# First four weight pieces of a fused attention and MoE kernel: loads issued twelve steps ahead, one conversion turn per step instead of three, and the read of the result moved one turn behind its last step

## The chip, the cores and the metric

One core of a Trainium2 chip (trn2). The metric is the device time of one execution in microseconds, taken over several runs of the same program.

## The reference

```python
def reference(**kwargs):
    attn_out = _attn_ref(q, k, v, proj)                 # (2, 8, 768, 64)
    x = attn_out.transpose(0, 2, 1, 3).reshape(1536, 512)
    x = _moe_ref(x, w_in, w_out)                        # h = x @ w_in ; (h * sigmoid(h)) @ w_out
    return _moe2_ref(x, w_in2, w_out2)                  # h = x @ w_in2 ; (h - tanh(h)) @ w_out2

def _attn_ref(q, k, v, proj):
    q_bucket, k_bucket = hash(q, proj), hash(k, proj)   # six sign bits of q @ proj, k @ proj
    mask = q_bucket[:, :, :, None] == k_bucket[:, :, None, :]
    scores = np.where(mask, q @ k.T / 8, -1e9)
    attn = exp(scores - max); attn = attn / (attn.sum(-1) + 1e-9)
    return attn @ v
```

Two batches, eight heads, 768 rows of 64 in each head; two feed-forward layers of 512 by 2048 and 2048 by 512. The feed-forward weights come as 64-bit floats and are used as 32-bit ones.

## The kernel before

Attention runs in tiles: a tile is 128 query rows of one head against all 768 keys, six tiles to a head, 96 in all. A generator (`attention`) walks through 122 steps, 61 for each batch: in a step it records the scores of one tile (`scores`, L243), the reduction of those scores from PSUM with a row maximum (`soft_max`, L256, one for each tile, so that its 96 instructions count the tiles), the exponential (`soft_exp`, L264 and L265), and the product with V of a tile six steps back (`pv`, L312 to L314). The tile is turned for that product either on TensorE (`turn_p`, L279, with L281 and L282 out of PSUM; the odd tiles of the first batch) or by a transposing DMA (`soft_hi` L291, `soft_lo` L298 on GpSimd, L300 on the queue of SyncE, called SP). Each step yields three times. Step 61 begins the second batch; the last thirteen steps of a batch have no new tile.

Every float32 operand of a matmul is held as a high and a low half, made by a cast on ScalarE and a subtraction on GpSimd or VectorE. Feed-forward weights come in pieces of 128 rows by 512 columns. `Moe.load` issues the DMA of one piece on SP (L467, 512 KB, a ring of two buffers `w`). `Moe.take` lists the steps that turn the 64-bit numbers into 32-bit ones, one lambda each, as "turns": an absolute value on ScalarE (L507), then L508, L509, L511 on VectorE, and a last turn `last` with L498 on VectorE, L499 on ScalarE (cast to `wh`), L500 on GpSimd (`wl`) and a store for later use on SP (L502). `Moe.fill` does n turns, after it has issued the loads that have come due (one for each piece finished). The scratch `wa` has two buffers.

The main loop (L647 to L655) puts this between the steps of attention. At step 33 (`half - PRE`, 61 - 28) it calls `begin`, which issues the first two loads, and starts `first_weights`, which takes the first four pieces; from then on it does one turn at each of the three yields of a step until the end of step 60. These four pieces are all the rows of the first chunk of the first layer, which the first matmul groups of that layer read (`h_group`, L531). From step 61 on attention and the feed-forward layers (`run`, L531 and L555) are interleaved, with six turns to a step; after attention the rest of the layers follows.

The program is recorded in this order and then scheduled: Tile orders the instructions of each engine by priority and dependence, and each engine and the SP queue work through their own list strictly in order. `keep_in_program_order` ties single instructions (L467, L507) to the order of recording.

## Time and profile before

| what | value |
|---|---|
| runs | 779.87, 783.84, 785.07 us; median 783.84 us |
| profiled execution | 781.58 us, span 779.8 us |
| TensorE busy (PE) | 728.1 us, 93% of the span |
| VectorE (DVE) | 541.5 us, 69% |
| ScalarE (ACT) | 432.0 us, 55% |
| GpSimd (POOL) | 306.2 us, 39% |
| mean granted TensorE clock | 0.982 |

The profile names engines PE (matmul), PEld (weight load), DVE, ACT, POOL and SP (SPq is the DMA queue of SP). Times in a view are us from the start of the span. An arrow `[2.32 <-DMA w...]` behind an instruction is the idle time of its engine just before it and what ended that. The page's slices show TensorE nearly full from the eleventh of forty slices (195 us) on, and busy between four and nine tenths in the first ten.

### The profile page before, as it was taken

The numbers are of one execution on the slowest core, as the hardware profiler recorded it, in microseconds if no ns is written. First come the engines' busy times: TensorE is split into PE (matmuls) and PEld (weight loads), VectorE is DVE, ScalarE is ACT, GpSimd is POOL, SyncE is SP. The second block draws the span as 40 slices with busy tenths as digits, with TensorE's granted clock in tenths as the row PEclk, the third lists the DMA queues.
The fourth block names the chain that finished last, engine by engine and source line by source line (L and its number), as shares of the span: only waits on it lengthen the run. The fifth ranks groups of instructions, "written<-read, shape, count | busy, mean of one in ns | idle before, by whom it ended". The sixth has DMA issues, their size and how long they took to land.

```text
span 779.8 us, 14314 instructions
## 1 busy us (share of the span) xinstructions
PE 728.1 (93%) x5492; PEld 698.0 (90%) x5492; DVE 541.5 (69%) x1029; ACT 432.0 (55%) x821; POOL 306.2 (39%) x214
## 2 busy tenths in 40 slices
PE   4688876798999999999999999999999999999998
PEld 3677775687989899999999999999999999999998
DVE  6778879698888888886442445996858567584342
ACT  3778867898788789666444332562524325242130
POOL 4455546566777768557454310221111111110000
PEclk8799999999999999999999999999999999999999
DMA  7756669689899999993233220332112121110102
GB/s 259 191 137 140 135 138 187 149 167 246 215 238 277 227 232 253 201 240 103 80 109 107 72 65 16 121 109 82 54 55 82 55 82 54 56 55 1 58 24 82
DMA packets 138879, 100.39 MB, mean 129 GB/s; under 512 B 115870, under 2 KB 118174, under 8 KB 138810
## 3 DMA queue, kind: packets, MB, share of 16 engines
q1 hardware_dynamic: 137712, 97.54, 49.5%
q10 hardware_dynamic: 1098, 1.94, 1.0%
q8 instruction: 43, 0.70, 0.4%
q14 instruction: 26, 0.21, 0.1%
HBM read 57.95 MB, written 11.53 MB: 89 GB/s over the span
## 4 chain that ended last, share of the span: by engine, by line
PE 55%; POOL 1%; DVE 0%; ACT 0%; issue 0%; ACTq 0%
PE psm L555 27%; PE psm L531 27%; POOL xl L579 1%; POOL wl L500 0%; PE pso L312 0%; PE pso L314 0%; PE pso L313 0%; DVE p L256 0%; DVE wa L498 0%; DVE xt L330 0%; DVE acc L567 0%; ACT xh L578 0%; DVE den L321 0%; DVE den L320 0%; ACTq L578 0%
## 5 line engine op out<-in xcount | busy, mean ns | idle before, releaser
L500 POOL TENSOR_TENSOR wl<-wa,wh 128x512 fp32r<-128x512 f32 x64 | 82.7, 1293 | 237.8 <-ACT wh L499 236.4
L531 PE MATMUL psm<-xh,wh 128*128 128x384 f32 x512 | 173.0, 338 | 1.0 <-DVE hb L185 0.5
L555 PE MATMUL psm<-gh,wh 128*128 128x384 f32 x512 | 173.0, 338 | 0.4 <-ACT x L347 0.4
L531 PE MATMUL psm<-xh,wl 128*128 128x384 f32 x512 | 171.4, 335 | 1.1 <-POOL wl L500 1.1
L555 PE MATMUL psm<-gh,wl 128*128 128x384 f32 x512 | 171.6, 335 | 0.6 <-POOL wl L500 0.6
L555 PE MATMUL psm<-gl,wh 128*128 128x384 f32 x512 | 171.8, 335 | 0.0
L531 PE MATMUL psm<-xl,wh 128*128 128x384 f32 x512 | 171.3, 335 | 0.0
L298 POOL TENSOR_TENSOR hl<-p,hl 128x768 f16<-128x768 f32 x72 | 119.5, 1660 | 90.1 <-ACT hl L291 78.0
L256 DVE TENSOR_SCALAR_CACHE_REDUCE p<-ps 128x768 f32<-128x768 f32 x96 | 90.7, 948 | 28.0 <-PE ps L243 23.6
L543 DVE TENSOR_TENSOR gl<-psm,gh 128x384 fp32r<-128x384 f32 x128 | 71.1, 556 | 41.9 <-ACT gh L542 41.6
L531 PEld LDWEIGHTS psm<-xh,wh 128*128 128x128 f32 x512 | 96.1, 188 | 1.6 <-DVE hb L185 0.6
L531 PEld LDWEIGHTS psm<-xh,wl 128*128 128x128 f32 x512 | 96.1, 188 | 1.5 <-POOL wl L500 1.5
L555 PEld LDWEIGHTS psm<-gh,wl 128*128 128x128 f32 x512 | 96.3, 188 | 0.9 <-POOL wl L500 0.9
L555 PEld LDWEIGHTS psm<-gh,wh 128*128 128x128 f32 x512 | 96.5, 189 | 0.7 <-ACT x L347 0.6
L243 PE MATMUL ps<-k,q 128*128 128x384 f32 x336 | 84.5, 371 | 13.5 <-DVE p L256 9.6
L555 PEld LDWEIGHTS psm<-gl,wh 128*128 128x128 f32 x512 | 96.5, 189 | 0.0
L531 PEld LDWEIGHTS psm<-xl,wh 128*128 128x128 f32 x512 | 96.2, 188 | 0.0
L567 DVE TENSOR_TENSOR acc<-acc,psm 128x384 f32<-128x384 f32 x96 | 52.5, 549 | 60.4 <-PE psm L555 59.4
L542 ACT CAST gh<-psm 128x384 fp32r<-128x384 f32 x128 | 61.4, 481 | 57.9 <-DVE psm L541 35.6
L265 ACT ACTIVATE p<-p,bi 128x768 f32<-128x768 f32 x96 | 89.1, 937 | 4.9 <-DVE xt L330 1.1
L243 PEld LDWEIGHTS ps<-k,q 128*128 128x128 f32 x336 | 62.1, 205 | 18.1 <-DVE p L256 10.9
L540 ACT ACTIVATE th<-psm 128x384 f32<-128x384 f32 x64 | 31.5, 493 | 75.6 <-PE psm L531 75.6
(104 smaller groups left out, 1275.9 us busy)
## 6 DMA issues: line engine op xcount, KB each, us to landing
w<-in_w_in_dram SPq DMA_DIRECT2D x32, 512.0 KB
w<-in_w_out_dram SPq DMA_DIRECT2D x32, 512.0 KB
r<-in_qkT_dram SPq DMA_DIRECT2D x15, 768.0 KB
wi<-wa SPq DMA_DIRECT2D x16, 256.0 KB
wo<-wa SPq DMA_DIRECT2D x16, 256.0 KB
w<-wi SPq DMA_DIRECT2D x16, 256.0 KB
w<-wo SPq DMA_DIRECT2D x16, 256.0 KB
vr<-in_v_dram SPq DMA_DIRECT2D x6, 512.0 KB
```

The lines of the kernel that those rows point to most:

```text
L243: nc.tensor.matmul(out=ps[:, u, 0:HS], lhsT=a[:, t * 128:(t + 1) * 128], rhs=c[:, u * HS:(u + 1) * HS], start=(j == 0), stop=(j == 1))
L256: nc.vector.tensor_scalar(p.rearrange("p (c s) -> p c s", c=2), pss.pop(i)[:, :, 0:HS], FLOOR, None, op0=ALU.max, op1=ALU.max, accum_out=m)
L265: nc.scalar.activation(out=p, in_=p, func=ACTF.Exp, scale=0.125, bias=bi)
L298: nc.gpsimd.tensor_tensor(hl[:, 1, :], p, hl[:, 0, :], op=ALU.subtract)
L500: nc.gpsimd.tensor_tensor(ll, s, hh.bitcast(F32), op=ALU.subtract)
L531: nc.tensor.matmul(out=ps, lhsT=a[:, k, fs], rhs=b_[blk][:, k, :], start=(k == 0 and j == 0), stop=(k == KD - 1 and j == 2))
L540: nc.scalar.activation(out=th, in_=ps, func=ACTF.Tanh)
L542: nc.scalar.copy(gh[:, f, :], ps)
L543: nc.vector.tensor_tensor(gl[:, f, :], ps, gh[:, f, :].bitcast(F32), op=ALU.subtract)
L555: nc.tensor.matmul(out=ps, lhsT=a[:, f, ds], rhs=b_[:, f, :], start=(f == 0 and j == 0), stop=(f == F - 1 and j == 2))
L567: nc.vector.tensor_tensor(ac, ac, ps, op=ALU.add)
L579: nc.gpsimd.tensor_tensor(xl[blk][:, dt, :], src, xh[blk][:, dt, :].bitcast(F32), op=ALU.subtract)
```

## The change

Three edits. The step L498 leaves `last` and becomes a turn of its own, so a piece has six turns, and its reads (cast, subtraction, store) are the sixth. `begin` is called twelve steps earlier, at step 21. And turns are done at the third yield of a step alone, so one to a step and not three. After step 60 nothing is edited, except that a piece has six turns there too.

```diff
             def last():
-                nc.vector.scalar_tensor_tensor(r, lo, 29, u, op0=ALU.logical_shift_right, op1=ALU.bitwise_or)
                 nc.scalar.copy(hh, s)
                 nc.gpsimd.tensor_tensor(ll, s, hh.bitcast(F32), op=ALU.subtract)
                 if dr is not None:
@@
                 lambda: nc.vector.scalar_tensor_tensor(u, hi, -0x40000000, u, op0=ALU.bitwise_and,
+                                                       op1=ALU.bitwise_or),
+                lambda: nc.vector.scalar_tensor_tensor(r, lo, 29, u, op0=ALU.logical_shift_right,
                                                        op1=ALU.bitwise_or),
                 last,
@@
         for s, sub in attn:
+            if s == half - PRE - 12 and sub == 0:
+                moe.begin()
             if s == half - PRE and sub == 0:
-                moe.begin()
                 pre = moe.first_weights()
-            if pre is not None:
+            if pre is not None and sub == 2:
                 next(pre, None)
                 moe.fill()
```

In the changed file the lines shift: L507, L508, L509, L511, L498, L499, L500, L502 become L506, L507, L508, L510, L512, L498, L499, L501, and L531 becomes L532.

What the scheduler makes of it. First VectorE, from tile 35 on: `wa` and `w` are the weight pieces, `p` and `psm` tiles of attention. Before:

```order
L256 TENSOR_SCALAR p,mx<-ps 128x768
L282 TENSOR_TENSOR p<-psm,p 128x384
L508 TENSOR_SCALAR wa<-wa 128x512
L330 TENSOR_TENSOR xt<-pso,den 128x6x64
L509 TENSOR_SCALAR wa<-wa 128x512
L256 TENSOR_SCALAR p,mx<-ps 128x768
L511 SCALAR_TENSOR_TENSOR wa<-w,wa 128x512
L256 TENSOR_SCALAR p,mx<-ps 128x768
L498 SCALAR_TENSOR_TENSOR wa<-w,wa 128x512
L508 TENSOR_SCALAR wa<-wa 128x512
```

And after the change, from the same place:

```order
L256 TENSOR_SCALAR p,mx<-ps 128x768
L282 TENSOR_TENSOR p<-psm,p 128x384
L330 TENSOR_TENSOR xt<-pso,den 128x6x64
L256 TENSOR_SCALAR p,mx<-ps 128x768 x2
L507 TENSOR_SCALAR wa<-wa 128x512
L508 TENSOR_SCALAR wa<-wa 128x512
L282 TENSOR_TENSOR p<-psm,p 128x384
L510 SCALAR_TENSOR_TENSOR wa<-w,wa 128x512
L282 TENSOR_TENSOR p<-psm,p 128x384
L512 SCALAR_TENSOR_TENSOR wa<-w,wa 128x512
L256 TENSOR_SCALAR p,mx<-ps 128x768 x2
L282 TENSOR_TENSOR p<-psm,p 128x384 x2
```

Up to the reduction of tile 47 sixteen such rows stood in the list before, and eight stand there now. The other eight now stand around the first tiles of the second batch, VectorE again (`hl` is a tile, `cv` the next piece's scratch):

```order
L282 TENSOR_TENSOR p<-psm,p 128x384 x2
L507 TENSOR_SCALAR wa<-wa 128x512
L508 TENSOR_SCALAR wa<-wa 128x512
L510 SCALAR_TENSOR_TENSOR wa<-w,wa 128x512
L256 TENSOR_SCALAR p,mx<-ps 128x768
L512 SCALAR_TENSOR_TENSOR wa<-w,wa 128x512
L282 TENSOR_TENSOR hl<-psm,hl 128x384 x3
L256 TENSOR_SCALAR p,mx<-ps 128x768
L282 TENSOR_TENSOR hl<-psm,hl 128x384
L507 TENSOR_SCALAR wa<-wa 128x512
L256 TENSOR_SCALAR p,mx<-ps 128x768
L508 TENSOR_SCALAR wa<-wa 128x512
```

The first reduction here is that of tile 48, the first of the second batch; before, none of the weight rows stood here. The queue of SP, before, from the load of a head's q and k (`r`) that is issued at 72.07:

```order
L134 DMA r<-in_qkT_dram 128x1536
L300 DMA_TRANSPOSE pt<-hl 128x12x128 x3
L134 DMA r<-in_qkT_dram 128x1536
L300 DMA_TRANSPOSE pt<-hl 128x12x128 x4
L467 DMA w<-in_w_in_dram 128x1024 x2
L300 DMA_TRANSPOSE pt<-hl 128x12x128
L502 DMA wi_75<-wa 128x512
L467 DMA w<-in_w_in_dram 128x1024
```

And after, from the same load on:

```order
L134 DMA r<-in_qkT_dram 128x1536
L300 DMA_TRANSPOSE pt<-hl 128x12x128
L467 DMA w<-in_w_in_dram 128x1024 x2
L300 DMA_TRANSPOSE pt<-hl 128x12x128 x2
L134 DMA r<-in_qkT_dram 128x1536
L300 DMA_TRANSPOSE pt<-hl 128x12x128 x6
L501 DMA wi_75<-wa 128x512
L467 DMA w<-in_w_in_dram 128x1024
L300 DMA_TRANSPOSE pt<-hl 128x12x128 x3
L501 DMA wi_75<-wa 128x512
L300 DMA_TRANSPOSE pt<-hl 128x12x128
L134 DMA r<-in_qkT_dram 128x1536
```

The two loads have moved past six transpositions and a head's load, to between two transpositions; the fourth load follows behind the last row shown. On TensorE one place ahead of that changes with it: the matmuls that wait for the transposition behind the two loads. Before:

```order
L314 LDWEIGHTS p
L314 MATMUL pso<-v_221,p 128x65
L312 LDWEIGHTS pt
L312 MATMUL pso<-v_221,pt 128x65
L313 LDWEIGHTS pt
```

After:

```order
L314 MATMUL pso<-v_221,p 128x65
L243 MATMUL ps<-k_644,q_642 128x384 x2
L243 MATMUL ps<-k_645,q_643 128x384 x2
L243 MATMUL ps<-k_644,q_642 128x384 x2
L312 LDWEIGHTS pt
L312 MATMUL pso<-v_221,pt 128x65
```

Three rows of score matmuls (L243), which stood behind the eighteen matmuls that read `pt`, now stand ahead of them.

## Rows read from the trace of the kernel before

**Rows 1.** Windows of the span: stretch, length, busy us by engine (count), PEclk, DMA share, GB/s.
```profile
60.00:105.00 45.00, 40.15 (x515) 34.46 (x514) 35.20 (x79) 38.06 (x77) 26.96 (x16) 1.00 0.63 124
105.00:140.00 35.00, 22.63 (x260) 18.91 (x258) 31.70 (x56) 25.01 (x47) 17.66 (x12) 0.90 0.79 184
...
200.00:350.00 150.00, 146.20 (x1424) 137.35 (x1423) 126.13 (x250) 120.67 (x214) 108.31 (x70) 1.00 1.03 236
350.00:779.00 429.00, 425.42 (x2468) 424.34 (x2466) 257.02 (x460) 161.24 (x326) 93.22 (x74) 1.00 0.22 69
```
**Rows 2.** Timeline of VectorE: reductions of tiles 24, 35, 36, 47, 48; start, length.
```profile
77.97 0.92 DVE L256 TENSOR_SCALAR_CACHE_REDUCE p<-ps 128x768 f32<-128x768 f32 x1
...
101.31 0.95 DVE L256 TENSOR_SCALAR_CACHE_REDUCE p<-ps 128x768 f32<-128x768 f32 x1
...
106.02 0.92 DVE L256 TENSOR_SCALAR_CACHE_REDUCE p<-ps 128x768 f32<-128x768 f32 x1
...
142.83 0.94 DVE L256 TENSOR_SCALAR_CACHE_REDUCE p<-ps 128x768 f32<-128x768 f32 x1
...
150.26 0.96 DVE L256 TENSOR_SCALAR_CACHE_REDUCE p<-ps 128x768 f32<-128x768 f32 x1 [4.59 <-PE ps L243]
```
**Rows 3.** Instructions by line, VectorE, 105 to 140: count | busy, mean ns | idle before.
```profile
L498 DVE SCALAR_TENSOR_TENSOR wa<-w,wa 128x512 int32<-128x512 int32 x4 | 6.0, 1497 | 0.0
L511 DVE SCALAR_TENSOR_TENSOR wa<-w,wa 128x512 int32<-128x512 int32 x4 | 5.0, 1253 | 0.0
L509 DVE TENSOR_SCALAR wa<-wa 128x512 int32<-128x512 int32 x4 | 2.9, 713 | 0.0
L508 DVE TENSOR_SCALAR wa<-wa 128x512 f32<-128x512 f32 x4 | 2.3, 578 | 2.2 <-ACT wa L507 2.2
```
**Rows 4.** Instructions by line, ScalarE, 105 to 140.
```profile
L507 ACT ACTIVATE wa<-w 128x512 f32<-128x512 f32 x4 | 2.7, 664 | 2.3 <-DMA w<-in_w_in_dram 2.3
L499 ACT CAST wh<-wa 128x512 fp32r<-128x512 f32 x4 | 2.5, 618 | 6.6 <-DVE wa L498 6.6
```
**Rows 5.** Instructions of the tile wa to 320 us: count, shortest/median/longest ns, starts.
```profile
L508 DVE TENSOR_SCALAR wa<-wa x4: 415/496/906, 109.6 to 129.2; 128x512 f32<-128x512 f32 x4
L509 DVE TENSOR_SCALAR wa<-wa x4: 415/670/1097, 110.4 to 131.0; 128x512 int32<-128x512 int32 x4
L511 DVE SCALAR_TENSOR_TENSOR wa<-w,wa x4: 680/1176/1980, 111.6 to 132.3; 128x512 int32<-128x512 int32 x4
L498 DVE SCALAR_TENSOR_TENSOR wa<-w,wa x4: 674/1641/2031, 113.1 to 134.7; 128x512 int32<-128x512 int32 x4
```
**Rows 6.** Timelines of VectorE and of GpSimd, one pair that runs at once.
```profile
113.12 2.03 DVE L498 SCALAR_TENSOR_TENSOR wa<-w,wa 128x512 int32<-128x512 int32 x1
...
112.95 1.65 POOL L298 TENSOR_TENSOR hl<-p,hl 128x768 f16<-128x768 f32 x1 [7.66 <-ACT hl L291]
```
**Rows 7.** Timeline of the DMA issues of SP.
```profile
77.17 1.44 SPq L300 DMA_TRANSPOSE pt<-hl  x1
...
104.46 1.11 SPq L467 DMA_DIRECT2D w<-in_w_in_dram  x2
```
**Rows 8.** Timeline of TensorE.
```profile
81.97 0.20 PE L312 MATMUL pso<-v,pt 128*128 128x65 f16 x1 [0.83 <-DMA pt<-hl]
...
143.86 0.43 PE L531 MATMUL psm<-xh,wh 128*128 128x384 f32 x1
...
148.97 0.20 PE L312 MATMUL pso<-v,pt 128*128 128x65 f16 x1 [1.53 <-DMA pt<-hl]
```
**Rows 9.** Two more windows, columns as in rows 1.
```profile
108.00:110.00 2.00, 0.00 (x0) 0.00 (x0) 0.38 (x2) 0.66 (x1) 0.00 (x0) 1.00 1.01 342
...
158.00:170.00 12.00, 10.91 (x85) 10.30 (x84) 11.36 (x27) 12.00 (x22) 6.11 (x7) 1.00 1.10 205
```
**Rows 10.** Timeline of VectorE behind tile 48.
```profile
155.65 0.96 DVE L256 TENSOR_SCALAR_CACHE_REDUCE p<-ps 128x768 f32<-128x768 f32 x1 [0.98 <-PE ps L243]
...
157.28 0.23 DVE L320 TENSOR_SCALAR den<-pso,vsc 128x6 f32<-128x6 f32 x1 [0.66 <-PE pso L314]
```

## What the change will do: the prediction

> **What bounds the kernel now.** I read the windows first, then the reductions of the score tiles as a clock of the pace, then who works and who waits where the pace breaks. Behind 200 us TensorE is the bound: 146.2 of 150 us busy, then 425.4 of 429 [rows 1]. Whatever happens earlier shifts that part as a block, since all five engines' orders are the same again from about 204 us on (the places shown above all lie ahead of it). So the question is what the change does up to there.
>
> In 60:105 TensorE is busy 40.15 of 45 us, in 105:140 only 22.63 of 35, while VectorE has 31.70 of 35 [rows 1]. The pace says the same: from the score reduction of tile 24 to that of tile 35 it is 23.34 us (77.97 to 101.31), from tile 36 to tile 47, again eleven tiles on, 36.81 us (106.02 to 142.83) [rows 2]. I call these the undisturbed pace and the stretch; the stretch loses 13.5 us to it. All four first weight pieces are converted in it: 16 VectorE instructions, 6.0 + 5.0 + 2.9 + 2.3 = 16.2 us [rows 3]. VectorE is the bound there; its only long wait is 2.2 us ahead of the first conversion, for ScalarE [rows 3], and ScalarE itself waits 2.3 us for the load of the weights [rows 4]. Between tiles 47 and 48 (7.43 us, "the gap") VectorE idles 4.59 us [rows 2]: the batches change and few tiles are at hand.
>
> **The change, part by part.** The working is against the profiled execution, 781.58 us, which lies 2.26 us under the median of the three runs, 783.84. As the new time will be a median too, I start from the middle, 782.7.
>
> (a) Loads twelve steps earlier. Both loads are issued at 104.46 [rows 7]; the wait behind them is the 2.2 us of VectorE [rows 3]. In the new order they stand just ahead of the transposition issued at 77.17 [rows 7], some 27 us earlier. The wait goes: -2.2. TensorE's clock was granted at 0.90 on average in 105:140 [rows 1], mostly the 2.4 GHz level and for a part 1.2 GHz, but TensorE is not the bound there, so I count nothing for it; if VectorE stops covering it, it is worth at most 0.10 x 22.63 = 2.3 us.
>
> (b) One conversion turn per step (every third of the old turns). The order of VectorE shows what that does: ahead of tile 47's last work stand eight conversion instructions, not sixteen. Two of four pieces leave the stretch. At the mean of the sixteen, 16.2 / 4 = 4.05 us a piece, that is -8.1. Bounds: if the two that stay cost the shortest of each kind, 0.415 + 0.415 + 0.680 + 0.674 = 2.18 us [rows 5], the stretch loses 16.2 - 4.4 = 11.8; if they cost the longest, 0.906 + 1.097 + 1.980 + 2.031 = 6.01, it loses 16.2 - 12.0 = 4.2. What makes the difference is seen in one pair: the last step at 113.12 takes 2.03 us while a GpSimd subtraction runs from 112.95 for 1.65 us [rows 6], against 0.674 at the shortest [rows 5]. GpSimd's work is the same as before, so I keep the mean. With (a) the stretch comes to 36.8 - 2.2 - 8.1 = 26.5 us, still over the undisturbed 23.3, so nothing of the sum runs into that floor.
>
> The Trainium skill (SBUF — State Buffer, "Who interferes with whom") states that a VectorE instruction with two SBUF inputs and a GpSimd one that reads SBUF block each other fully; the pair at 113.12 agrees. By that rule alone a slower cadence saves only if the steps miss the subtractions, and the sum would be as likely -6.0 + 3.9 = -2.1 (4.2 instead of 8.1) as -6.0 - 3.7 = -9.7 (11.8).
>
> (c) The two pieces land in the gap and just behind it. The order puts three steps of the third piece ahead of tile 48's reduction, the fourth step behind it, and the fourth piece around tiles 49 to 51. Cover there: 4.59 us [rows 2] plus 0.98 and 0.66 [rows 10], 6.2 us. At the mean, 8.1 - 6.2 = +1.9. Behind it, in 158:170, ScalarE is busy 12.00 of 12.00 us [rows 9], and one cast of 0.618 us [rows 4] comes close ahead of it: +0.6. So +2.5. Bounds: without crowding only what stands between reductions and is not covered, 0.674 for the third piece's last step and 0.415 + 0.680 + 0.674 for the fourth piece's steps behind tile 50, less 0.98 + 0.66 [rows 5, 10], +0.8; at the longest 12.0 - 6.2 + 0.6 = +6.4.
>
> (d) The two early loads now stand directly ahead of the transposition issued at 77.17 [rows 7], for whose result TensorE already waits 0.83 us at 81.97 [rows 8]. 1.05 MB at the 342 GB/s of 108:110 [rows 9] is 3.1 us. Bounds 0 and +3.1. In the new order TensorE has three rows of score matmuls ahead of that wait that stood behind it, so VectorE's next reductions do not wait with it: I take a third, +1.0.
>
> The Trainium skill (DMA: Bandwidth & Descriptors, "Queues, rings and completion order") has each DMA engine consume one queue's descriptors in ring order. That is the argument against this part: by it the transposition is late by the full 3.1.
>
> (e) The fourth load stands ahead of one of the last transpositions of the batch, on which TensorE waits at 148.97 (1.53 us) [rows 8]: 0.52 MB at the same rate is 1.5 us; bounds 0 and +1.5, I take +0.8, as part of TensorE's wait there is also on others.
>
> (f) The read of the result one turn later. ScalarE's four casts wait 6.6 us for the step ahead of them [rows 4]; in the new order a dozen rows stand between. VectorE was the busy one through those waits (31.70 of 35 us, [rows 1]), so they are covered and I count nothing; without that cover they would be a gain of up to 6.6. In the later pieces the last step and its read come out of the same call (three turns at once), and the order there is the old one: nothing.
>
> Sum: -2.2 - 8.1 + 2.5 + 1.0 + 0.8 = -6.0; 782.7 - 6.0 = **776.7 us**.
>
> **The rivals.**
> *Everything hides.* The conversion sits in idle time of VectorE, and the stretch returns to the undisturbed pace, 23.34. For it: VectorE has 35.20 of 45 us busy in 60:105 [rows 1], so 9.8 us are free per 45. Against: those holes come while TensorE is ahead, and the turns stand between reductions in the order. Price: -13.5 + 0.8 from (c) + 0 = -12.7, 770.0 us.
> *The stalls only change place.* The wait for the load comes back as the wait for the transposition in full (+3.1 against -2.2), and the pieces that stay are as crowded as the longest (-4.2), with the moved ones at +1.9 + 0.6 and (e) +0.8. Together 0.0: 782.7 us, no change. For it: TensorE's wait at 81.97 [rows 8], which has no reserve. Against: the three rows of score matmuls in (d), and the mean of the sixteen. The rule of the Trainium skill in (d) would bring about the first half of this case.
> *Slower: the fourth piece is late.* Before, all four pieces were converted in 105:140 [rows 3], and the first group that reads them starts at 143.86 [rows 8]. Now the fourth load needs the second piece's last step, and on SP it stands behind a transposition and the load of the next head; ScalarE's first step of that piece stands ahead of its exponentials, so a late load holds all of attention, as at 104.46 [rows 7], and TensorE's third and fourth weight triples stand in its queue ahead of score matmuls. Ahead of it 0.79 + 0.52 MB at 342 GB/s take 3.8 us; the room is the gap of 7.43 us plus the 2.5 us or so to tile 50. From 6 us of lateness on, the gain is gone; from 14 us the kernel is over 1% slower. With 8 us it is 785 us. Against: ScalarE's wait for the two first loads, issued with no lead at all, was 2.3 us [rows 4].
>
> **How the numbers follow.** Chances: the sum as worked out (773 to 780) 0.47, everything hides 0.17, stalls change place 0.24, fourth piece late 0.12. The bounds of all terms give -2.2 - 11.8 + 0.8 = -13.2 (held by the floor of the pace at about 770) and -2.2 - 4.2 + 6.4 + 3.1 + 1.5 = +4.6 (787). The range that leaves about 2 in 10 outside is 770.5 to 784.0; the likeliest case alone has 773 to 780. One per cent, 7.8 us, is about what a measurement here can tell from no change. Faster by more: all of the first rival and about two fifths of the sum's own range, 0.17 + 0.19 = 0.36. Slower by more: a good half of the last rival, 0.07. Within: 0.57.
>
> **What would show it.** (a): no wait of ScalarE on the weight load ahead of the first conversion. (b): tiles 36 to 47 in 25 to 29 us, with eight conversion instructions between. (c): VectorE's idle time ahead of tile 48 mostly filled, tiles 48 to 60 no longer than before. (d): TensorE's wait on the transposition near 82 us grows to about 4 us, while the next two reductions keep their time. (e): the wait near the end of the batch stays under 3 us. (f): no waits of the casts. The forecast is wrong if the stretch keeps over 31 us, if ScalarE waits for the third or fourth load, or if the part behind 204 us does not keep its length.

## The result, and the profile after

The changed kernel takes 790.3 us (median of 14 runs, 785.6 to 795.5) against 784.4 us (14 runs, 779.9 to 786.4) beside it: a ratio of 1.0084, interval 1.0064 to 1.0104. It is slower by 0.84%, which lies within the one per cent, but on the other side of the forecast and above its range. The profiled execution took 790.33 us (span 788.5, mean granted clock 0.976), 8.75 us more than the one of before.

First the windows of the changed kernel, columns as in [rows 1].

```profile
60.00:105.00 45.00, 35.98 (x450) 30.92 (x449) 30.50 (x68) 33.75 (x65) 22.94 (x14) 0.92 0.71 136
105.00:140.00 35.00, 29.04 (x367) 24.87 (x366) 31.65 (x61) 29.24 (x60) 17.92 (x12) 0.95 0.61 109
...
200.00:350.00 150.00, 146.18 (x1391) 137.35 (x1390) 126.53 (x250) 120.02 (x212) 108.01 (x70) 1.00 1.03 236
```

Behind 200 us nothing is new: TensorE is as full as before. In 60:105 TensorE is busy 4.2 us less than in [rows 1]; in 105:140 it is busy 6.4 us more, with VectorE as busy as before (31.65 against 31.70 us). The reductions (L256), counted as in [rows 2], say where the time went; the numbers are differences of their starts in the two profiled executions.

| from reduction to reduction | before | after | difference |
|---|---|---|---|
| tile 0 to 24 | 61.29 | 60.66 | -0.6 |
| tile 24 to 36 | 28.05 | 33.96 | +5.9 |
| tile 36 to 47 | 36.81 | 27.18 | -9.6 |
| tile 47 to 48 | 7.43 | 12.48 | +5.05 |
| tile 48 to 60 | 52.74 | 59.37 | +6.6 |
| tile 60 to 95 | 132.37 | 132.91 | +0.5 |
| tile 95 to the end of the span | 444.43 | 445.25 | +0.8 |

So the stretch gave what it was to give, and three places around it took 17.6 us. The first is the early loads. Timelines of the changed kernel: SP's queue, TensorE and VectorE.

```profile
75.25 1.42 SPq L467 DMA_DIRECT2D w<-in_w_in_dram  x2
76.78 7.28 SPq L300 DMA_TRANSPOSE pt<-hl  x2
...
86.88 0.23 PE L312 MATMUL pso<-v,pt 128*128 128x65 f16 x1 [5.23 <-DMA pt<-hl]
...
89.61 0.96 DVE L256 TENSOR_SCALAR_CACHE_REDUCE p<-ps 128x768 f32<-128x768 f32 x1 [6.84 <-PE ps L243]
```

The transposition issued at 76.78 is used at 86.88, 10.1 us later. Before, the one issued at 77.17 [rows 7] was used at 81.97 [rows 8], 4.8 us later. TensorE stands still for 5.2 us instead of 0.8, and VectorE's next reduction comes after 6.8 us of idling. Windows of five us show what TensorE does behind such a wait; here and at the two later places.

```profile
75.00:80.00 5.00, 4.28 (x57) 3.72 (x57) 4.64 (x13) 3.13 (x7) 1.53 (x1) 1.00 1.04 238
80.00:85.00 5.00, 1.65 (x24) 1.29 (x19) 2.77 (x8) 5.00 (x8) 3.88 (x3) 0.87 1.24 183
85.00:90.00 5.00, 3.12 (x35) 3.03 (x36) 0.39 (x1) 0.08 (x1) 2.95 (x2) 0.50 1.18 214
...
145.00:150.00 5.00, 1.22 (x20) 1.14 (x19) 1.33 (x3) 3.79 (x6) 3.92 (x2) 0.85 0.60 114
150.00:155.00 5.00, 3.85 (x17) 2.90 (x17) 3.63 (x7) 1.00 (x2) 0.56 (x1) 0.50 0.30 68
...
160.00:165.00 5.00, 0.98 (x9) 0.73 (x6) 4.97 (x10) 3.71 (x8) 4.19 (x5) 1.00 0.85 255
165.00:170.00 5.00, 5.00 (x25) 4.97 (x24) 3.60 (x11) 3.60 (x8) 3.96 (x3) 0.66 1.07 241
```

Where TensorE was busy 1.65 of 5 us, the next five have a granted clock of 0.50, the 1.2 GHz level; the same again behind 1.22 of 5 in 145:150. In 160:165 it is busy 0.98 us, this time with VectorE full (4.97 of 5); there the granted clock is still 1.00, and 0.66 in the next five.

The second place is the end of the batch, answering to [rows 8]: SP's queue, TensorE, VectorE.

```profile
140.69 0.43 SPq L467 DMA_DIRECT2D w<-in_w_in_dram  x1
142.75 1.81 SPq L300 DMA_TRANSPOSE pt<-hl  x1
...
148.87 0.24 PE L312 MATMUL pso<-v,pt 128*128 128x65 f16 x1 [3.78 <-DMA pt<-hl]
...
150.97 0.96 DVE L256 TENSOR_SCALAR_CACHE_REDUCE p<-ps 128x768 f32<-128x768 f32 x1 [4.57 <-PE ps L243]
```

The same transposition in SP's queue of the kernel before:

```profile
144.43 1.66 SPq L300 DMA_TRANSPOSE pt<-hl  x1
```

The fourth load stands ahead of the last transposition of the batch, which is used 6.1 us after its issue; before it was 4.5 us (issue at 144.43, use at 148.97 [rows 8]). Although three steps of the third piece now stand in VectorE's list ahead of tile 48 (1.55 us, from 144.79 on), VectorE idles 4.57 us there, as much as before (4.59, [rows 2]).

The third place is between the reductions of tiles 50 and 51: VectorE, GpSimd and TensorE.

```profile
157.20 0.96 DVE L256 TENSOR_SCALAR_CACHE_REDUCE p<-ps 128x768 f32<-128x768 f32 x1 [0.54 <-PE ps L243]
158.08 1.23 DVE L508 TENSOR_SCALAR wa<-wa 128x512 int32<-128x512 int32 x1
159.34 0.69 DVE L510 SCALAR_TENSOR_TENSOR wa<-w,wa 128x512 int32<-128x512 int32 x1
160.06 2.01 DVE L512 SCALAR_TENSOR_TENSOR wa<-w,wa 128x512 int32<-128x512 int32 x1
162.00 0.69 DVE L507 TENSOR_SCALAR cv<-cv 128x512 f32<-128x512 f32 x1
162.73 0.69 DVE L508 TENSOR_SCALAR cv<-cv 128x512 int32<-128x512 int32 x1
163.43 0.92 DVE L256 TENSOR_SCALAR_CACHE_REDUCE p<-ps 128x768 f32<-128x768 f32 x1
...
159.57 1.96 POOL L298 TENSOR_TENSOR hl<-p,hl 128x768 f16<-128x768 f32 x1 [0.55 <-ACT hl L291]
...
164.41 0.97 PE L243 MATMUL ps<-k,q 128*128 128x384 f32 x4 [4.02 <-DVE p L256]
```

Five conversion steps of the fourth and fifth piece, 5.3 us, stand between the two reductions, one of them beside a GpSimd subtraction at 2.01 us; TensorE's next scores wait 4.0 us for the second. TensorE's waits in 135:205, by what it waited for (us in total, times, longest), for the changed kernel:

```profile
PE ps L243 <- DVE p L256: 8.1, 5, 4.0
PE pso L312 <- DMA pt<-hl: 6.6, 3, 3.8
```

The same view of the kernel before has 3.5 and 2.6 us.

What the change was made of shows as it should. Instructions by line, ScalarE in 105:140 and VectorE in 111:140 of the changed kernel, answering to [rows 4] and [rows 3]:

```profile
L506 ACT ACTIVATE wa<-w 128x512 f32<-128x512 f32 x2 | 1.3, 674 | 0.7 <-issue 0.7
L498 ACT CAST wh<-wa 128x512 fp32r<-128x512 f32 x2 | 1.2, 617 | 0.0
...
L510 DVE SCALAR_TENSOR_TENSOR wa<-w,wa 128x512 int32<-128x512 int32 x2 | 3.0, 1490 | 0.0
L508 DVE TENSOR_SCALAR wa<-wa 128x512 int32<-128x512 int32 x2 | 2.8, 1382 | 0.0
L512 DVE SCALAR_TENSOR_TENSOR wa<-w,wa 128x512 int32<-128x512 int32 x2 | 2.7, 1353 | 0.0
L507 DVE TENSOR_SCALAR wa<-wa 128x512 f32<-128x512 f32 x2 | 0.8, 423 | 0.0
```

No wait for the load and none of the casts; two pieces, 9.3 us of VectorE, where four took 16.2.

### The profile page after: what moved, and what is told of

The parts are those of the page before. It is cut to its first block, busy times and chain, and to the rows that moved or that the text cites. A ratio compares the mean times of both kernels' runs of the same rounds, so it can differ in the third digit from the quotient of the medians.

```text
span 788.5 us, 14311 instructions
## 1 busy us (share of the span) xinstructions
PE 731.3 (93%) x5492; PEld 700.2 (89%) x5492; DVE 543.0 (69%) x1029; ACT 432.0 (55%) x821; POOL 306.8 (39%) x214
## 4 chain that ended last, share of the span: by engine, by line
PE 46%; DMA 4%; POOL 3%; ACT 1%; DVE 1%; issue 1%; DVEq 0%; POOLq 0%; ACTq 0%
PE psm L556 25%; PE psm L532 21%; POOL wl L486 2%; DMA w<-wi 2%; DMA w<-wo 2%; POOL xl L580 1%; ACT wh L485 1%; DMA w<-in_w_out_dram 0%; POOL wl L499 0%; ACT wh L498 0%; DVE cv L507 0%; DVE cv L510 0%; DVE psm L539 0%; DVE cv L508 0%; DVE wa L512 0%
## 5 line engine op out<-in xcount | busy, mean ns | idle before, releaser
L499 POOL TENSOR_TENSOR wl<-wa,wh 128x512 fp32r<-128x512 f32 x64 | 82.7, 1292 | 239.3 <-ACT wh L498 239.3
L532 PE MATMUL psm<-xh,wh 128*128 128x384 f32 x512 | 173.9, 340 | 0.5 <-DVE gl L544 0.5
L532 PE MATMUL psm<-xh,wl 128*128 128x384 f32 x512 | 171.6, 335 | 1.0 <-POOL wl L499 1.0
L532 PE MATMUL psm<-xl,wh 128*128 128x384 f32 x512 | 171.7, 335 | 0.0
L256 DVE TENSOR_SCALAR_CACHE_REDUCE p<-ps 128x768 f32<-128x768 f32 x96 | 90.7, 949 | 32.8 <-PE ps L243 27.3
L243 PE MATMUL ps<-k,q 128*128 128x384 f32 x336 | 85.9, 375 | 14.5 <-DVE p L256 9.7
L532 PEld LDWEIGHTS psm<-xh,wl 128*128 128x128 f32 x512 | 96.4, 188 | 1.4 <-POOL wl L499 1.4
L532 PEld LDWEIGHTS psm<-xh,wh 128*128 128x128 f32 x512 | 96.5, 188 | 1.1 <-DVE gl L544 0.9
L532 PEld LDWEIGHTS psm<-xl,wh 128*128 128x128 f32 x512 | 96.5, 188 | 0.0
L243 PEld LDWEIGHTS ps<-k,q 128*128 128x128 f32 x336 | 62.7, 206 | 18.7 <-DVE p L256 11.1
```

What stands on the lines that cost most here:

```text
L243: nc.tensor.matmul(out=ps[:, u, 0:HS], lhsT=a[:, t * 128:(t + 1) * 128], rhs=c[:, u * HS:(u + 1) * HS], start=(j == 0), stop=(j == 1))
L256: nc.vector.tensor_scalar(p.rearrange("p (c s) -> p c s", c=2), pss.pop(i)[:, :, 0:HS], FLOOR, None, op0=ALU.max, op1=ALU.max, accum_out=m)
L499: nc.gpsimd.tensor_tensor(ll, s, hh.bitcast(F32), op=ALU.subtract)
L532: nc.tensor.matmul(out=ps, lhsT=a[:, k, fs], rhs=b_[blk][:, k, :], start=(k == 0 and j == 0), stop=(k == KD - 1 and j == 2))
```

## The experiments

The expectations of the first runs name two theories: A puts the loss on the place of the early loads on SP, B on the slower conversions. D, E and V are narrower: loads ahead of an awaited transposition; the fourth load's place; the third and fourth piece on VectorE in the gap. From here on "the gap" is the whole change of batch, from tile 47 to about tile 51, and not tiles 47 to 48 alone. Every run's ratio is to runs of the kernel before on the same chip. The columns are differences of the starts of L256 in the one profiled execution of each.

| run | ratio, interval | span | 24 to 36 | 36 to 48 | 48 to 60 | 60 to 72 |
|---|---|---|---|---|---|---|
| before | 1 | 779.8 | 28.05 | 44.24 | 52.74 | 44.84 |
| after | 1.0084 (1.0064, 1.0104) | 788.5 | 33.96 | 39.66 | 59.37 | 46.63 |
| e1_early | 1.0027 (1.0003, 1.0050) | 784.9 | 33.01 | 42.66 | 51.29 | 44.88 |
| e4_late | 1.0090 (1.0061, 1.0119) | 789.1 | 27.99 | 43.87 | 61.75 | 45.29 |
| e5_ten_ahead | 1.0015 (0.9981, 1.0049) | 786.4 | 28.60 | 39.86 | 61.81 | 46.98 |
| e6_two_turns | 0.9935 (0.9904, 0.9965) | 776.3 | 28.47 | 42.14 | 50.73 | 45.56 |
| e7_hold | 1.0017 (0.9992, 1.0041) | 781.5 | 28.25 | 38.27 | 59.43 | 45.29 |
| e8_front | 1.0089 (1.0055, 1.0122) | 786.7 | 29.12 | 38.60 | 58.13 | 49.45 |
| e9_free | 0.9987 (0.9967, 1.0007) | 777.8 | 28.61 | 41.00 | 51.18 | 47.12 |
| e10_one_ahead | 1.0040 (1.0012, 1.0067) | 788.7 | 33.01 | 38.04 | 61.23 | 47.17 |
| e11_spread | 0.9982 (0.9959, 1.0005) | 782.3 | 34.70 | 35.99 | 52.73 | 47.06 |
| e12_skip | 0.9997 (0.9973, 1.0020) | 781.9 | 28.34 | 39.85 | 54.74 | 49.40 |
| e13_split | 0.9996 (0.9970, 1.0022) | 784.1 | 27.92 | 46.78 | 51.78 | 47.08 |
| e14_pause | 1.0004 (0.9984, 1.0025) | 780.4 | 28.48 | 37.86 | 61.16 | 45.56 |
| e15_three | 0.9969 (0.9950, 0.9989) | 775.8 | 28.47 | 41.29 | 50.72 | 45.53 |
| e16_two_again | 0.9981 (0.9961, 1.0001) | 778.8 | 29.00 | 42.20 | 51.21 | 45.47 |
| e17_both | 0.9990 (0.9967, 1.0012) | 785.8 | 28.63 | 39.30 | 56.60 | 48.59 |

A caution for reading it: a trace is one execution, and executions of one kernel differ by some 4 us either way (e5: 780.4 to 789.4). Sizes of whole-kernel effects are taken from the ratios; the columns say where an effect sits.

**The place of the loads.** e1_early is the kernel before with the loads at step 21 and nothing else:

```diff
+            if s == half - PRE - 12 and sub == 0:
+                moe.begin()
             if s == half - PRE and sub == 0:
-                moe.begin()
```

> The kernel before with one edit alone: the first two loads at step 21 and not 33; three turns per step and the old last turn stay. In the order of SP the two loads stand between the first and the second transposition behind a head's load, as in the changed kernel. Theory A (the loads push the transposition that TensorE waits for, and the loss is never won back): about 7 us lost at tiles 27 to 30 as in the changed kernel, 2 to 3 us won at tile 36 where the wait for the load is gone: 4 to 5 us slower than before, ratio about 1.006. Theory B (the loss of the changed kernel comes from the weight pieces that moved into the change of batch; what is lost near 80 us is slack of the stretch that follows): 2 us faster than before, ratio 0.997.

1.0027, between what A and B asked. Tiles 24 to 36 lose 5.0 us as in the changed kernel. Timelines of e1_early, SP's queue and TensorE:

```profile
76.63 1.39 SPq L467 DMA_DIRECT2D w<-in_w_in_dram  x2
78.14 7.36 SPq L300 DMA_TRANSPOSE pt<-hl  x2
...
87.58 0.20 PE L312 MATMUL pso<-v,pt 128*128 128x65 f16 x1 [4.36 <-DMA pt<-hl]
```

e4_late is the changed kernel with `begin` back at step 33.

```diff
-            if s == half - PRE - 12 and sub == 0:
-                moe.begin()
             if s == half - PRE and sub == 0:
+                moe.begin()
```

> The changed kernel with the two loads back at step 33: one turn per step and the split last turn stay. Theory A: no wait of 5 us near 82 us; what the changed kernel lost there, 7 us, comes back, the wait of ScalarE for the load (2 us) returns; 4 to 6 us under the changed kernel, ratio to before about 1.002. Theory B: as slow as the changed kernel, ratio about 1.008 or more.

The place at 24 to 36 is back to 27.99 us, and yet the kernel is no faster than the changed one, 1.0090: A alone is not enough. Without the early loads the stretch has its load wait again (ScalarE waits 2.2 us), and 48 to 60 takes 61.75 us. e5_ten_ahead is the changed kernel with the loads two steps later; on SP they then stand behind one more transposition, the one (issued at 77.24) that TensorE waits for near 82 us.

```diff
-            if s == half - PRE - 12 and sub == 0:
+            if s == half - PRE - 10 and sub == 0:
```

> The changed kernel with the loads ten steps ahead instead of twelve. In the order of SP they then stand between the second and the third transposition behind a head's load, where the DMA engines of the old kernel were idle (82 to 84 us), and nothing else in the order of SP changes. Theory A: the wait near 82 us is back under 1.5 us, nothing else changes, 7 us under the changed kernel: about the time of before, ratio 0.999. Theory B: as slow as the changed kernel, ratio 1.008.

24 to 36 costs 28.60 us, and the ratio falls from 1.0084 to 1.0015. One place of difference on the queue, for a prefetch that is awaited nowhere, is worth 0.69%, or 5.4 us. e9_free does the same to the kernel before (e1's edit with 10 for 12).

> The kernel before with one edit: the first loads ten steps ahead, behind the two transpositions that TensorE waits for, all conversions as before. This is term a alone, without the cost that the twelve-step place showed. Theory of the prediction: no wait for a load at tile 36, 36 to 47 takes 34.4 us instead of 36.8, everything else as before: span 777.4, ratio 0.997. Rival (early loads cost wherever they stand in the stretch, since they share the DMA engines with the transpositions): 24 to 36 grows by 2 us or more, ratio 1.000 or above.

0.9987, with the expected 0.997 just inside its interval, and 777.8 us of span (777.4 expected); from e1 to e9 the place is worth 0.40%, 3.1 us. So 3 to 5 us of the loss are the place of the loads, shown twice. e10_one_ahead (e5's edit with 8 for 10) gives the dose. Its timelines, SP's queue and TensorE:

```profile
75.69 0.86 SPq L467 DMA_DIRECT2D w<-in_w_in_dram  x1
77.06 2.80 SPq L300 DMA_TRANSPOSE pt<-hl  x1
...
84.20 0.23 PE L312 MATMUL pso<-v,pt 128*128 128x65 f16 x1 [3.17 <-DMA pt<-hl]
```

> The changed kernel with its first loads eight steps ahead: by the order on SP one load stands ahead of a transposition on either side, spread over the places behind the second and third transposition, instead of two in a row. A dose between twelve steps ahead (tiles 24 to 36 in 33.96 us) and ten (28.60). Theory D (TensorE waits in proportion to the load bytes ahead of the transposition that it waits for): 24 to 36 takes 30 to 32 us. Rival (only two loads in a row ahead of the first transpositions after a head's load cost, one hides): 28 to 29 us. The rest as with ten steps ahead: 36 to 47 in 27.2 us, 47 to 48 in 12.6, span 786 to 789.

From issue to use the transposition takes 4.8 us with no load ahead of it (before), 7.1 with one and 10.1 with two (9.4 in e1): some 2.3 to 3 us for 512 KB. The delay goes in proportion, as D says; the segment does not (33.01 us, above the 30 to 32 expected). The second load now stands ahead of the transposition after that, but so do both in e5, which loses nothing there. Windows from tile 24 to tile 36, columns as in [rows 1]: the kernel before, the changed one and e10.

```profile
77.97:106.02 28.05, 24.90 (x322) 21.45 (x322) 21.67 (x50) 24.36 (x49) 17.09 (x10) 1.00 0.62 122
...
77.35:111.31 33.96, 26.42 (x322) 22.91 (x322) 21.78 (x50) 24.55 (x49) 16.98 (x10) 0.90 0.71 130
...
77.87:110.88 33.01, 27.36 (x322) 23.81 (x322) 21.85 (x49) 24.53 (x49) 16.98 (x10) 0.90 0.66 133
```

The same 322 matmuls keep TensorE busy 2.5 us longer in e10 than before, and 1.5 us longer in the changed kernel, with the lower granted clock behind the wait. So of the 4.4 us that e10 loses to e5 about half is the longer wait (3.17 us against 0.98) and about half the slower clock behind it. Two more things hold for e10. Its loads are recorded two steps later than e5's, and yet the first of them stands ahead of the awaited transposition again in the order that the scheduler made: the place on the queue decides, not the step. And its ratio can't be told from e5's, as the intervals overlap; the dose is read from the traces alone.

**The slower conversions.** e6_two_turns is e5 with two turns to a step, so that all four pieces end before the gap again.

```diff
-            if pre is not None and sub == 2:
+            if pre is not None and sub:
```

> As the one with ten steps, but two turns per step instead of one, so that all four pieces are converted, and the fourth load issued, ahead of the last transpositions of the batch. If the change of batch costs what the traces say (tile 47 to 60 about 11 us longer than before in the changed kernel, by the fourth load ahead of a transposition and by the pieces converted there), this takes most of these 11 us away and gives back up to 8 us in the stretch from tile 36 to 47, so about 3 us under the version with one turn, ratio to before about 0.995. If the pieces there are hidden by idle time, it is slower than the version with one turn by up to 8 us, ratio 1.005 to 1.01.

0.9935 and faster than both kernels; 48 to 60 takes 50.73 us. Against it e15_three (`if pre is not None:`, all three turns) and e16_two_again (the kernel of e6 once more), side by side:

> Loads ten steps ahead, the result read one turn later, and all three turns of a step used as before: the changed kernel without its slower conversions. Theory (the four pieces end before the gap, so the gap costs what it did before; a and f alone change): 36 to 47 in 34 us, 47 to 48 in 7.3, 48 to 60 in 51 us, span 776 to 778.5, ratio 0.994 to 0.998. Rival (two turns per step are better by themselves, since a piece delays each reduction less): 781 us or more here, ratio 0.998 or above, and 0.9935 again with two turns.

> The same kernel as the run with two turns per step, with more rounds and beside the one with three. Theory (the pace inside the stretch moves nothing as long as all four pieces end before tile 47): ratio within 0.2 percent of the one with three turns, both 0.994 to 0.998. Rival: 0.9935 here and 0.998 or above with three.

0.9969 and 0.9981: no difference between two and three turns that these runs can tell, and the 0.9935 of e6 (7 runs) did not come again in 12. What holds of it is a gain of about 0.3% over the kernel before. In e15 tiles 36 to 48 take 41.29 us, the 41.3 expected, but split otherwise: 47 to 48 takes 4.69 us and not 7.3. TensorE's waits in 135:205 in e15:

```profile
PE ps L243 <- DVE p L256: 3.0, 4, 1.2
PE pso L312 <- DMA pt<-hl: 1.6, 2, 0.9
```

They are those of before, not those of after. With the loads at one place, one turn per step (e5, 1.0015) costs 0.46% or 3.6 us against three (e15, 0.9969), though the intervals, taken on two chips, leave it anywhere between under 1 and over 6 us; with the loads late, e4 against e13, it is 0.94%, 7.4 us. That is the second cause. In the traces it sits in 48 to 60, which takes 59 to 62 us in all runs with one turn per step and whole pieces in the gap (58.13 in e8, whose first two pieces are converted faster), and 51 to 53 in all runs in which four pieces end before it.

e13_split is the kernel before with the first two pieces of the change's diff alone: L498 leaves `last` and becomes a turn of its own.

> The kernel before with the result's read (copy, subtraction and store) one turn behind the last conversion step, and nothing else: term f alone, for all pieces of the whole kernel. The prediction counts it as 0: span within 2 us of 779.8, ratio 0.998 to 1.002. Rival (a turn more per piece spreads the first four pieces over two tiles more and puts their last reads later: the first feed-forward products wait): 48 to 60 rises by 1 to 3 us, ratio 1.002 to 1.004.

0.9996: (f) is nothing, as counted, to within the 2 us or so that the interval leaves. Its one trace missed the expected span (784.1), with TensorE waiting 3.15 us on the last transposition of the batch; the median did not follow it.

**What in the gap costs.** e7_hold is e5 with the fourth load withheld until step 47, behind the last transposition of the batch:

```diff
+            if not self.hold:
                 for _ in range(self.due):
                     self.load()
                 self.due = 0
@@
+                moe.hold = 44 <= s < 47
```

> The changed kernel with its first three loads ten steps ahead instead of twelve, and the fourth load's issue withheld until step 47, so that on SP it stands behind the last transposition of the second head half instead of ahead of it. To be compared with the run that has the loads ten steps ahead (786.4 us of span; tiles 47 to 48 took 12.65 us, 48 to 60 took 61.81). Theory E (the DMA order costs there: the load keeps the last transposition back, as in term e): 47 to 48 comes back to 8 to 9 us, TensorE's wait for pt near tile 48 falls from about 3.8 us to 1.5 or less, the span to about 782. Theory V (the place is slow since TensorE and VectorE have two weight pieces to carry there, whatever the DMA order): 47 to 48 and 48 to 60 stay within 1 us, span 785 to 788. If the load only hits another transfer, 48 to 60 grows by what 47 to 48 gives.

Timelines of e7, SP's queue and TensorE:

```profile
137.54 1.66 SPq L300 DMA_TRANSPOSE pt<-hl  x1
139.25 1.25 SPq L468 DMA_DIRECT2D w<-in_w_in_dram  x1
...
142.27 0.24 PE L312 MATMUL pso<-v,pt 128*128 128x65 f16 x1 [2.39 <-DMA pt<-hl]
```

The transposition is used 4.7 us after its issue instead of 6.3 in e5, so between these two traces the load's place is worth 1.6 us. But 47 to 48 only falls to 11.08 us (8 to 9 were expected by E), and the ratio does not move (1.0017). Nor is the load needed for a late transposition there. In e13 no weight load stands between it and the load of the next head's q and k (768 KB); in e11, told of below, all pieces are done before and none stands there either. Timelines of e13, SP's queue and TensorE, and then of e11:

```profile
143.18 0.57 SPq L134 DMA_DIRECT2D r<-in_qkT_dram  x1
144.62 10.38 SPq L300 DMA_TRANSPOSE pt<-hl  x2
...
152.22 0.20 PE L312 MATMUL pso<-v,pt 128*128 128x65 f16 x1 [3.15 <-DMA pt<-hl]
...
140.71 9.05 SPq L300 DMA_TRANSPOSE pt<-hl  x2
...
147.00 0.24 PE L312 MATMUL pso<-v,pt 128*128 128x65 f16 x1 [3.79 <-DMA pt<-hl]
```

It is used 7.6 and 6.3 us after its issue. The head's load stands ahead of it in every kernel, the one before too; no run moves that load, so its share in the wait is untested. E is at most a part of the wait, and not of the time that can be measured.

e12_skip leaves VectorE's steps of the third and fourth piece out of e5 but for 32 of 512 columns; all four steps are cut like the one shown.

```diff
+            q = slice(0, 32) if key in ((0, 0, 0, 2), (0, 0, 0, 3)) else slice(None)
...
-                lambda: nc.vector.tensor_scalar(t, t, W_MIN, W_MAX, op0=ALU.max, op1=ALU.min),
+                lambda: nc.vector.tensor_scalar(t[:, q], t[:, q], W_MIN, W_MAX, op0=ALU.max, op1=ALU.min),
```

> The changed kernel with its loads ten steps ahead, and of the third and fourth piece the four VectorE steps cover 32 of 512 columns only (the rest of these two pieces stays unconverted; loads, ScalarE and GpSimd steps and the stores stay as they are). Theory V (VectorE's conversion steps in the gap delay the reductions that TensorE waits for): 47 to 48 falls from 12.65 to 8 to 9.5 us, 48 to 60 from 61.8 to 52 to 55 us, span 775 to 779. Theory E (it is the fourth load and the stores among the transpositions and head loads): 47 to 48 stays at 11 us or more and 48 to 60 above 58 us, span 782 to 786.

A split answer. 47 to 48 stays at 12.63 us as E wants, 48 to 60 falls by 7.1 us as V wants, and 60 to 72 is 2.4 us longer than in e5; the ratio is 0.9997. TensorE's waits in 135:205 of e12:

```profile
PE pso L312 <- DMA pt<-hl: 8.0, 4, 3.9
PE ps L243 <- DVE p L256: 1.2, 1, 1.2
```

The wait for the reduction is mostly gone (7.1 us in e5), the waits for transpositions are all there (7.6 in e5). e17_both takes both away (e7's and e12's edits together):

> One turn per step, loads ten steps ahead, fourth load withheld until step 47, and the VectorE steps of the third and fourth piece on 32 of 512 columns (these two pieces stay unconverted for the rest). If the load's place and the VectorE steps are the two causes and they add: 47 to 48 about 11 us, 48 to 60 52 to 54 us, span 773 to 777, ratio 0.988 to 0.995. If something else holds the gap (stores, ScalarE and GpSimd steps of the two pieces, or TensorE's lower granted clock after a wait that stays): 48 to 60 56 us or more, span 779 to 783, ratio 0.998 or above.

They do not add: 48 to 60 takes 56.60 us, the ratio is 0.9990. That is the outcome that was given to something else in the gap, which no run singles out. e14_pause is e5 with no turns in steps 45 to 50 and two to a step from step 51 on:

```diff
-            if pre is not None and sub == 2:
+            if pre is not None and (sub == 2 and not 45 <= s < 51 or sub == 1 and s >= 51):
```

> The changed kernel with its loads ten steps ahead, no conversion turn in steps 45 to 50, and two turns per step from step 51 on: the last two pieces keep out of the place where the heads change, and are converted behind it; the fourth load is issued there too. Theory V: 47 to 48 falls from 12.65 to 7.5 to 9 us, and 48 to 60 to 54 to 58 us, as the pieces still come ahead of the first feed-forward products; span 779 to 783. Rival (what costs is that the pieces come late, wherever VectorE does them, since the first feed-forward products have to wait for them): 48 to 60 stays at 61 us or more, span 784 to 788.

47 to 48 falls to 11.09, but 48 to 60 stays at 61.16, as the rival has it; the ratio, 1.0004, is between the two. TensorE's waits in 135:205 of e14:

```profile
PE pso L312 <- DMA pt<-hl: 4.8, 3, 3.0
PE psm L532 <- ACT wh L498: 2.8, 1, 2.8
PE psm L556 <- POOL wl L499: 1.9, 1, 1.9
```

Now the first feed-forward products wait for the pieces themselves. So the traces show three costs in the gap that take each other's place: converting there makes reductions late, converting behind it makes the weights late, and TensorE waits for transpositions that are late. Which share each has in the time is open: e5, e7, e12, e14 and e17 lie between 0.9990 and 1.0017, within each other's intervals. Only finishing the pieces ahead of the gap brought 48 to 60 back to 51 to 53 us.

**Two attempts to keep part of it.** e8_front does two turns per step in the first six steps and then one; e11_spread begins the conversions six steps sooner, with a second turn in each third step, so that all four end before the gap. The lines that differ from e5, e8's first and then e11's two:

```diff
+            if pre is not None and (sub == 2 or (sub == 1 and half - PRE <= s < half - PRE + 6)):
...
+            if s == half - PRE - 6 and sub == 0:
                 pre = moe.first_weights()
+            if pre is not None and (sub == 2 or (sub == 1 and s % 3 == 0)):
```

> The loads ten steps ahead, and two conversion turns per step in the first six steps of the stretch, one from then on. The first two pieces end three tiles sooner, and the third and fourth move ahead by as much. Theory V (what costs is third and fourth pieces that stand at tiles 48 to 51, where the attention's next head begins): 48 to 60 falls from 61.8 us by 2 to 5 us, 36 to 47 rises from 27.2 by 2 to 4 us, span 783 to 786. Theory E (the fourth load's place by the last transposition): the fourth load has moved ahead by several transpositions here, so 47 to 48 falls to 8 or 9 us, and the span is 781 to 783 at most 784.

> Loads ten steps ahead (the free place), the conversions begun six steps sooner, with one turn per step and a second one in every third step: about 18 steps for the four pieces instead of 28 (changed) or 9 (before), and all of them done before the gap at tiles 47 to 51. Theory V (a piece is nearly free among the steps of the second head half when it comes a step at a time, and dear in the gap): tiles 24 to 47 take 60 to 62 us together (55.8 with two pieces in them in the run with ten steps, 62.8 with four in the run with two turns), 47 to 48 7.5 to 8.5 us, 48 to 60 51 us, span 773 to 777, ratio 0.988 to 0.994. Rival (the pieces cost VectorE time wherever they are, so that spreading them gives nothing over two turns per step): span 777 to 780, ratio 0.994 to 0.998.

Both missed. e8 gains 3.7 us in 48 to 60 against e5, and 60 to 72 takes 2.5 us more; at 1.0089 (four runs) it is the slowest with the changed kernel and e4. In 60 to 72 TensorE waits 3.2 us once for VectorE (`xt`, L330), at a mean granted clock of 0.93 where e5 has 1.00; why is open (inconclusive). In e11 48 to 60 takes 52.73 us, as without pieces, and 36 to 48 only 35.99, but 24 to 36 rises by 6.1 us against e5: from tile 24 to 48 it takes 70.69 us, and 69.76 in e15, so spreading the pieces over more tiles saved nothing. And 47 to 48 takes 12.66 us, not the 7.5 to 8.5 expected, although no piece and no fourth load is left in the gap. Where tile 47's reduction comes 1.8 us behind tile 46's, as here and in the changed kernel, 47 to 48 is 11 to 12.7 us in every trace: the reductions have run ahead, and the next batch still waits for the last transposition.

## Why the prediction was wrong, step by step

Everything behind tile 60 held: the last two rows of the first table are +0.5 and +0.8 us. The starting point, 782.7, was 1.7 us under the 784.4 us measured beside the changed kernel; the other 11.9 of the 13.6 us by which the forecast missed lie in the terms. The slower conversions were to gain 4.8 us ((b), (c) and (e): -8.1 + 2.5 + 0.8) and cost 3.6 (e15 to e5) or 7.4 (e13 to e4). The early loads were to gain 1.2 us ((a) and (d)), and their place alone cost 3.1 to 5.4, against 1 to 2 us that the vanished load wait gave. None of the three signs named for a wrong forecast came: the stretch took 27.18 us, nothing waited for the third or fourth load, and the part behind 204 us kept its length. They looked at the stretch, and the time was lost around it.

- **(a), the load wait, -2.2: right.** No wait on the load in the changed kernel. From tile 36 to the issue of the last awaited transposition of the batch, e9 against before is 35.36 against 38.41 us, -3.05. In the ratio it is small: 0.9987 (e9), 1.0 us.
- **(b), two pieces out of the stretch, -8.1: right at the place that was read, wrong for the end.** VectorE's conversion time fell from 16.2 to 9.3 us, -6.9, and 36 to 47 by 9.6 us together with (a), against 10.3 expected. But what the second batch waits for is the last transposition of the first, and that was issued 31.44 us after tile 36 instead of 38.41: -7.0 for (a) and (b), 3.9 of it (b) (e9 35.36, e5 31.47), below the lower bound of 4.2. Tile 47's reduction ran ahead (1.8 us behind tile 46's, 5.55 before), and the time came back as TensorE's wait at 148.87. In e11, with neither pieces nor the fourth load behind tile 47, it came back as well (47 to 48 in 12.66 us, a wait of 3.79). The step that failed is the end point of the stretch: the chain behind the last reduction was not followed to the transposition. (a), (b) and (e) were to give -9.5 us from tile 36 to tile 48, and gave -4.6.
- **(d), the early loads, +1.0: mis-sized, and its upper bound too.** Tiles 24 to 36 lost 5.9 us against bounds of 0 and 3.1: 4.4 us of longer waiting for the transposition (5.23 against 0.83), and 1.5 us of slower matmuls behind it. The bound took the rate of 108:110 [rows 9], two us in which TensorE did nothing; here the engines moved 183 and 214 GB/s in 80:85 and 85:90, and the transposition was 5.3 us late, which for 1.05 MB is 198 GB/s (an estimate). Why the rate is lower here, no run tries. The Trainium skill (DMA: Bandwidth & Descriptors, "Queues, rings and completion order") has each DMA engine consume the descriptors of a queue in ring order. The argument drawn from it, "late by the full 3.1", was the right one in kind and too small in size; the dose of e10 (7.1 us with one load, 10.1 with two) agrees with the rule. The three rows of score matmuls taken for cover fed one more reduction, tile 27's, and no further: VectorE idled 6.84 us ahead of tile 28's.
- **(e), the fourth load, +0.8: near in the wait, not seen in the time.** From issue to use the transposition took 1.6 us longer than before, about the upper bound of 1.5; holding the load back restored it (e7, 4.7 us) without a gain in the ratio. As e11 and e13 show delays as long without that load, how much of the 1.6 us is the load's stays open. TensorE's wait, forecast at under 3 us, was 3.78.
- **(c), the pieces in the gap, +2.5: mis-sized.** 48 to 60 lost 6.6 us in this trace and 9 in e4 and e5, the upper bound being 6.4. The cover that was counted, VectorE's 4.59 us of idling ahead of tile 48, was not used: 4.57 us of idling stand there still. The fourth piece's last three steps come behind tile 50, in a place where TensorE waits for the next reduction; tiles 50 to 51 took 6.23 us instead of 2.46. Idle time in front of an instruction covers only what the order places there. The Trainium skill (SBUF — State Buffer, "Who interferes with whom") has a VectorE step with two SBUF inputs and a GpSimd one that reads SBUF block each other; the pair at 160.06 (2.01 us beside a subtraction) agrees, and such a step now stands on the path.
- **(f), 0: right** (e13, 0.9996, interval 0.9970 to 1.0022).
- **The clock, counted as nothing: wrong in its place.** In the stretch it rose (0.90 to 0.95). But behind the waits at 86.88 and 148.87 TensorE ran at the 1.2 GHz level for the next us, in which VectorE waited for it. Behind the first it cost 1.5 us, as TensorE was busy 26.42 us and not 24.90 with the same 322 matmuls. Behind the second it took 2.1 us instead of 1.3 from the use of the last transposition to tile 48. From tile 48 to 60 the matmuls are not the same ones (394 against 380), so the price there can't be read off; no run tried the clock by itself.

Of the rivals, "the stalls only change place" named the right kind of cause, with too small prices. "The fourth piece is late" ended on the right side by another mechanism: no instruction waited for the fourth load in the changed kernel; it was the reductions behind the conversions on VectorE and the transpositions that were late. Only where the pieces were put off further (e14) did the first products wait for weights.

Adding the traced parts, -0.6 + 5.9 - 9.6 + 5.05 + 6.6 + 0.5 + 0.8 = +8.7 us, the difference of the spans. Against the forecast sum of -6.0 that is 14.7 us, in three parts of nearly one size: 4.9 from (d), 4.1 from (c), 4.9 from the end of the stretch ((a), (b) and (e) together), and 0.7 elsewhere. By the ratios: about 3 to 5 us for the place of the loads and 4 to 7 for the slower conversions, less 1 to 2 for the load wait (e9, and e15 against e13), 5 to 11 together, which leaves room for the 0.84%, 6.6 us, that was measured.

## What to carry to other kernels

A prefetch is not free because nobody waits for it: find the next transfer on the same queue that an engine does wait for, and put the prefetch behind it; here standing behind one more transposition was worth 3 to 5 us. Read the place from the queue and not from the step at which the load is recorded (e10). When work leaves a stretch, measure the gain at the event on which the next stretch starts, not at the last instruction of the old one, and see which list the work lands in: idle time covers only what stands in the order right ahead of it. Best here was to take the free part alone: loads ten steps ahead and the conversions as fast as before, 0.9969 (0.9950 to 0.9989) of the time of the kernel before.

## What the runs showed of the hardware

The DMA transposition near 77 us was used 4.8, 7.1 and 10.1 us after its issue with none, one and two 512 KB loads right ahead of it on the queue, although the issue itself was not held back (76.78 against 77.17). The fourteen traces with none have 4.7 to 5.0 us, the other one with two (e1) 9.4. At the end of the batch the same kind of transposition took 4.4 to 7.6 us without a weight load behind the head's load (e9 and e13 the ends), so there the count of loads does not tell the delay. TensorE's granted clock stood at 0.50 in the five us behind a stretch in which it was busy 1.65 of 5 us, and again behind 1.22 of 5, but at 0.98 us busy in 160:165 it was still 1.00 and the mean of 165:170 was 0.66. The same 322 matmuls took 24.90 us of TensorE at a granted clock of 1.00 throughout, and 26.42 and 27.36 at a mean of 0.90. One kernel measured twice on two chips gave 0.9935 and 0.9981 against the same reference, with intervals that overlap by a hair; whether the chip or the number of runs (7 and 12) makes the difference is open.
